# Attention with mixture of experts: one PSUM ring for scores and maxima, two heads' maxima in one instruction, a fourth v buffer, a new order

## The chip, the cores and the metric

The kernel runs on one core of a Trainium2 chip. Its time is the device time of one execution in microseconds; before the change it was measured three times. Engines are named as in the profile: PE (matrix products; PEld is its weight load), DVE, ACT, POOL, and SP, which issues most of the transfers.

## The reference, cut

```
q_n, k_n = rmsnorm(q, g_q), rmsnorm(k, g_k)          # 8 x 12 heads, 448 tokens, 64 wide
scores = q_n @ k_n.T / 8
scores = scores - max(scores)
attn = exp(scores) / (sum(exp(scores)) + 1e-9)
x = reshape(attn @ v)                                # 3584 tokens x 768
e_idx = argmax(x @ w_gate)                           # one of 8 experts for each token
gate_w = softmax(x @ w_gate)[e_idx]; eom = sigmoid(x @ w_output_gate)
for e in range(8):
    mask = e_idx == e
    ye = relu(x[mask] @ w1[e]) @ w2[e]               # 768 -> 1024 -> 768
    out[mask] = gate_w[mask] * eom[mask, e] * ye
```

All of it is f32. The kernel keeps that accuracy by splitting factors into a high and a low f16 part and adding three f16 products.

## The kernel before, in words

**Attention** runs over 48 pairs of heads (8 batches of 6). `pair_ops(i)` lists the steps of pair `i`; a letter and a number is the name of a step in the tables. Lt loads q and k; sq, mh, ms, n, qg norm them; hi and lo split them into f16 parts, Th and Tl turn them by DMA transposes (`flip`) into `ss`. M0 to M3 (line 548) multiply the high parts alone, each head's block of 128 rows by 448 columns into a bank of PSUM, and x0 to x6 (line 556) take the maxima of rows on DVE into `Z`. NT turns Z on PE, nt copies it out. S0 to S3 are the exact scores less the maximum, in four units of keys; e, f and p make the exponentials on ACT and split them (`ph` on ACT, `pl` on POOL or DVE). A *whole* unit keeps one f32 exponential `pf` instead; `WHOLE` says how many a pair has, by the pair's number modulo 6. Lv loads v, vh and vl split it. A0 to A6 multiply with v: for whole units one f32 product, for others three f16 products. av1, av2, av divide by the sums, tr, th, lg, la feed the gate, and `route(b)` then sorts a batch's tokens by expert: the table `tab` and rows of x, `xs`, go to HBM. The last row of xs is blank, written once by k.xs; k.tab fills the table first.

**PSUM** has eight banks: `ps_m` three single banks, for M, NT, routing and the tails; `ps_s` two double banks, for S and the experts' products; `ps_a` one.

**Order.** `Order.run()` writes the program of attention and of the first expert. For each engine it takes, among the steps whose predecessors and buffers (`BUFS`) are ready at a planned time, the one with the lowest key; keys come from the tables `ORDER` (for each step, and by the remainder of the pair) and `SHIFT`, planned durations from the calls of `do` and `add`, and `SECOND` says in which pairs a step runs on its second engine. Each engine then works through its own list in that order. A step waits there, and all behind it, until its data are there.

**Experts.** Job e multiplies the tokens of expert e: a main part of 384 tokens and a tail. Tokens are gathered (`xge`), split by ACT and DVE (`x16e`) and turned by DMA transposes (`xTe`). `wstream` loads weights in six pieces a job (`wste`, three buffers) and splits each twice: high part w0he or w1he on ACT, low part on DVE. g1 is the first product, `he0h`/`he0l` its rounded and low part (`he0th`, `he0tl` in the tail), g2 the second. All 12 splits of job 1 stand in the planned part, that is, ahead of the tail of job 0; later ones are interleaved with the products by `wstep`:

```
def wstep(k):
    if splits and splits[0][0] == k + 1:
        m, x = splits.pop(0)
        for w in range(2):
            split(m, x, w)
        if x % 2 and loads:
            load(*loads.pop(0))
```

Of the kernel before, what the change touches and what calls it, by code (L numbers as in the profile page):

```python
# [22 lines left out]
E, F = 8, 1024  # L23
# [15 lines left out]
WHC = 1024  # L39
LGN = 2  # L40
# [4 lines left out]
BUFS = dict(m=3, s=2, a=1, p32=3, ph=3, pl=2, pf=2, ss=4, X=3, Z=3, nt=3, vh=3, vl=3, xT=4, sq=2, qkt=8, vf=3, ms=2, y=2, xg=2, x16=2, o=2, lg=2, rt=2, wst=3, ti=4)  # L45
# [3 lines left out]
    ("Lt", -47.506, -68.244, 168.634),  # L49
    ("sq", 302.855, -337.037, 75.045),  # L50
    ("mh", -605.679, -57.018, -151.507),
    ("ms", 295.539, 1280.387, 511.843),
    ("n", 76.337, -596.069, 411.443),
    ("qg", 3.274, -959.675, 293.592),
    ("hi", 220.1, -124.186, -353.622),
    ("Th", -96.148, 38.457, 271.519),
    ("lo", -200.856, -181.461, -607.745),
    ("Tl", -323.414, -550.546, 270.775),
    ("M0", -2.62, -24.949, -432.815),
    ("x0", -103.535, 25.55, -15.932),  # L60
    ("x4", 106.174, 131.323, -155.443),
    ("M1", -1.058, 0.342, -5.456),
    ("x1", -145.398, -78.771, -73.078),
    ("x5", -20.548, 262.928, -60.28),
    ("M2", -1.178, 1.859, 2.292),
    ("x2", -278.017, -206.72, -471.808),
    ("x6", -75.108, -103.324, 28.323),
    ("M3", -1.508, 330.302, -654.327),
    ("x3", 278.734, -108.242, -87.117),
    ("NT", -116.679, 2.458, 167.319),  # L70
    ("nt", 38.455, -342.151, -44.891),
    ("S0", 0.304, -0.032, -203.657),
# [12 lines left out]
    ("e3", -41.908, 331.636, 270.381),
    ("f3", 191.382, 481.021, -45.813),
    ("p3", -148.41, 311.486, -229.907),
    ("Lv", -0.418, -102.362, 203.578),
    ("vh", -222.505, -41.76, 172.536),
    ("vl", -110.713, 163.718, -1030.872),  # L90
    ("A0", 2.002, 263.597, 250.508),
    ("A1", -1.073, -322.948, 280.671),
    ("A2", -14.914, -632.993, 316.303),
    ("A3", -34.425, -48.666, -54.49),
    ("A4", 1.105, -437.479, -191.275),
    ("A5", 1.7, -0.098, 256.361),
    ("A6", 1.506, 0.301, 308.556),
    ("av1", -171.058, -1206.521, -141.056),
    ("av2", -106.328, 26.761, -592.507),
    ("av", -154.077, -642.22, -844.834),  # L100
    ("tr", -108.772, -139.57, -75.908),
    ("th", -228.323, -289.618, -1169.065),
    ("lg", 4.374, -1.236, 520.21),
    ("la", -239.437, -568.368, 565.533),
# [10 lines left out]
STICK = 0.027  # L115
# [15 lines left out]
    "p0": "100001 111101 001010",  # L131
    "p1": "110111 111110 000101",
    "p2": "100010 000000 101001",
    "p3": "110111 111001 011110",
    "lo": "100000 000000 110110",
    "vh": "000000 000000 011111",
    "th": "011111 000100 110101",
    "n": "110010 010100 011101",
    "qg": "100000 000011 110100",
    "nt": "110100 011011 000100",  # L140
}

WHOLE = (1, 1, 2, 2, 1, 1)
# [3 lines left out]
IN_TURN = ("hi", "Th", "vh", "th")  # L147

SHIFT = {
    "k.cst": -322.738,  # L150
    "k.gd": -238.947,
    "k.wg": 285.318,
    "k.blank": 152.09,
    "k.xs": 825.387,
    "k.tab": 400.65,
    "k.g": 296.375,
    "k.ltri": 502.271,
    "k.flat": -263.51,
    "k.edges": -261.446,
    "s0": -499.19,  # L160
    "r": 0.991,
    "st": -373.362,
    "s": 218.895,
    "r-2": -262.274,
    "r-1": -937.938,
    "open1": -790.202,
    "open2": -304.552,
    "ld0": 240.548,
    "wh0": 191.816,
    "wl0": 143.296,  # L170
    "ld1": -708.071,
    "wh1": -407.871,
    "wl1": 164.604,
    "ld2": 302.394,
    "ti0": 81.591,
    "xg0": 97.719,
    "xh0": 401.873,
    "xl0": -377.394,
    "xt0": -242.315,
    "ti1": -167.525,  # L180
    "xg1": -77.39,
    "xh1": 234.09,
    "xl1": 344.869,
    "xt1": -204.364,
    "ti2": -606.745,
    "xg2": -196.244,
    "xh2": -377.672,
    "xl2": 151.592,
    "xt2": -439.307,
    "units": 8.951,  # L190
    "g1": 764.664,
    "hh": 366.746,
    "hl": -393.214,
    "g2": 394.253,
    "o0": -88.676,
    "o1": 471.038,
    "sc": -498.536,
    "k.sel": 435.503,
# [118 lines left out]
class Kern:  # L317
# [12 lines left out]
    def consts(self):  # L330
# [3 lines left out]
        self.ps_m = self.pool("ps_m", 3, PSUM)  # L334
        self.ps_s = self.pool("ps_s", 2, PSUM)
# [24 lines left out]
        z = c.tile([128, KD], F32, name="zrow")  # L360
# [27 lines left out]
        add("k.wg", SP, 475, [], -5.5, load(self.wg, io["wg"]), (), 2000, 400)  # L388
        add("k.blank", POOL, 900, [], -8, blank)
        add("k.xs", SP, 475, ["k.blank"], -3.5, load(self.xs[NT : NT + 1, :].rearrange("o (k p) -> (o p) k", p=128), z), (), 2000, 336)  # L390
# [4 lines left out]
        add("k.tab", SP, 475, ["k.blank"], -3, table, (), 2000, 742)  # L395
# [89 lines left out]
    def pair_ops(self, i):  # L485
# [227 lines left out]
        do("Lt", SP, 475, "", lambda: self.stat_load(i), "qkt:lo", 1650, 1150)  # L713
# [11 lines left out]
        do("Th", SP, 1235, "hi", lambda: flip(0), f"ss:{Ss},M0,M1,M2,M3 Z:NT", 1650, 1215, more=["k.edges"])  # L725
        eng, ns = engine("lo")
        do("lo", eng, ns, "hi", lambda eng=eng: lo(eng))
        do("Tl", SP, 1235, "lo Th", lambda: flip(1), "", 1650, 1215)
        for k in range(4):
            js = (k, k + 4) if k < 3 else (3,)  # L730
            do(f"M{k}", PE, 195 if k < 3 else 210, "Th", lambda js=js: M(js), " ".join(f"m:x{j}" for j in js))
            for j in js:
                do(f"x{j}", DVE, 531, f"M{k}", lambda j=j: x(j))
# [402 lines left out]
    def product(self, q, nm):  # L1136

        if not q["tail"]:
            return self.ps_s.tile([128, 2, 512], F32, tag="s", name=nm)[:, :, 0 : q["n"]]
# [368 lines left out]
```

## Time and profile before

| | |
|---|---|
| median of 3 runs | 1059.21 us (1058.59 to 1063.82) |
| profiled execution | 1063.45 us, its span 1061.6 us |
| busy PE, PEld | 963.3 us (91% of the span), 680.8 us |
| busy DVE, ACT, POOL | 652.2, 558.9, 422.5 us |
| mean granted clock of PE | 0.969 |

The profiled execution is one of its own, 4.24 us above the median. Busy times are of the engine's own instructions; a matmul that runs beside another one on other rows of the array is counted once. A share of busy time over the whole span hides stretches with other limits, so the span is read in pieces: attention to about 505 us, the change-over to about 647, then the experts. Where an instruction had to wait, the trace names the engine and line, or the transfer, that released it.

### The profile page before, as it was taken

What the parts mean: (1) busy time and instruction counts of PE and PEld (TensorE: products, weight loads), DVE (VectorE), ACT (ScalarE), POOL (GpSimd) and SP (SyncE); (2) the same over time, 40 slices, a digit from 0 to 9 for tenths busy, and PEclk for the clock granted to TensorE, in tenths of its full rate; (3) what the DMA queues carried; (4) which work ended last, traced back from release to release, by engine and by line L of the source; (5) the groups of instructions that cost most, each with busy time, mean ns of one, the idle gap of its engine ahead of it and who ended that gap; (6) DMA issues with size and microseconds to landing.
All of it is one profiled execution on the core that took longest, in us unless ns stands there. A gap on an engine that the chain in (4) does not pass through costs nothing. (4 is left out here: it accounts for less than half of the span.)

```text
span 1061.6 us, 27539 instructions
## 1 busy us (share of the span) xinstructions
PE 963.3 (91%) x11800; PEld 680.8 (64%) x11800; DVE 652.2 (61%) x1201; ACT 558.9 (53%) x876; POOL 422.5 (40%) x337
## 2 busy tenths in 40 slices
PE   0789999999899999999879959989999899999997
PEld 0457776767667777777556556676676666666664
DVE  5897988797887987788745443616416144354310
ACT  5686878778677786665543433404325143343310
POOL 6885586777667666344421311121111200101001
PEclk9799999999999999999989969999999999999999
DMA  9656757557584674737583883743828538386301
GB/s 233 139 121 130 192 129 160 131 108 195 98 183 101 157 158 82 144 62 138 130 147 132 254 271 117 208 160 111 235 74 224 181 97 233 108 218 209 99 15 44
DMA packets 183309, 157.32 MB, mean 148 GB/s; under 512 B 153226, under 2 KB 161034, under 8 KB 177040
## 3 DMA queue, kind: packets, MB, share of 16 engines
q1 hardware_dynamic: 177136, 131.18, 51.4%
q0 software_dynamic: 6048, 24.35, 7.1%
q8 instruction: 94, 1.54, 0.6%
q14 instruction: 31, 0.25, 0.1%
HBM read 96.73 MB, written 22.59 MB: 112 GB/s over the span
## 5 line engine op out<-in xcount | busy, mean ns | idle before, releaser
L557 DVE TENSOR_REDUCE Z<-psM 128x1 f16<-128x448 f32 x336 | 196.3, 615 | 30.9 <-PE psM L554 26.8
L579 PE MATMUL pss<-ss 64*128 64x448 f16 (+1 forms) x1152 | 152.9, 370 | 13.3 <-ACT p L597 6.4
L636 PE MATMUL psa<-vf,pf 128*128 128x65 f32 (+1 forms) x1024 | 160.7, 276 | 2.6 <-issue 2.6
L605 POOL TENSOR_TENSOR pl<-p,ph 128x896 f16<-128x896 f32 (+1 forms) x67 | 115.0, 1717 | 81.1 <-ACT p L597 40.5
L636 PEld LDWEIGHTS psa<-vf,pf 128*128 128x128 f32 (+1 forms) x1024 | 121.0, 178 | 31.3 <-issue 23.8
L1172 POOL DMA_INDIRECT out<-oe,tie x24 | 29.8, 1240 | 259.2 <-DVE oe L1194 203.8
L601 ACT ACTIVATE ph<-pss 128x896 f16<-128x896 f32 (+1 forms) x128 | 97.7, 774 | 57.6 <-PE pss L585 51.8
L538 POOL TENSOR_TENSOR X<-qkt,X 128x512 f16<-128x512 f32 x86 | 102.8, 1219 | 57.5 <-ACT X L534 57.4
L1157 PE MATMUL g1e<-xTe,w0he 128*128 128x384 f16 x384 | 125.2, 326 | 0.0
L1159 PE MATMUL g1e<-xTe,w0le 128*128 128x384 f16 x384 | 125.2, 326 | 0.0
L1158 PE MATMUL g1e<-xTe,w0he 128*128 128x384 f16 x384 | 125.2, 326 | 0.0
L640 PE MATMUL psa<-vh,pl 128*128 128x65 f16 (+1 forms) x1024 | 118.4, 195 | 1.1 <-issue 1.1
L640 PE MATMUL psa<-vh,ph 128*128 128x65 f16 (+1 forms) x1024 | 118.1, 196 | 0.0
L638 PE MATMUL psa<-vl,ph 128*128 128x64 f16 (+1 forms) x1024 | 117.9, 193 | 0.0
L554 PE MATMUL psM<-ss 64*128 64x448 f16 (+1 forms) x384 | 80.0, 372 | 37.7 <-DMA ss<-X 24.6
L640 PEld LDWEIGHTS <-ph 128*128 128x128 f16 (+1 forms) x1024 | 105.4, 118 | 0.1
L585 PEld LDWEIGHTS <-sel 64*128 64x128 f16 (+1 forms) x1536 | 64.5, 101 | 36.2 <-issue 6.3
L640 PEld LDWEIGHTS <-pl 128*128 128x128 f16 (+1 forms) x1024 | 85.9, 101 | 1.2 <-issue 1.2
L638 PEld LDWEIGHTS <-ph 128*128 128x128 f16 (+1 forms) x1024 | 85.7, 103 | 0.0
L1158 PEld LDWEIGHTS <-w0he 128*128 128x128 f16 x624 | 61.8, 100 | 35.3 <-issue 11.7
L579 PEld LDWEIGHTS <-ss 64*128 64x128 f16 (+1 forms) x1152 | 50.2, 100 | 52.4 <-issue 19.9
L1157 PEld LDWEIGHTS <-w0he 128*128 128x128 f16 x624 | 61.7, 100 | 28.0 <-DMA xTe0t<-x16e0t 2.3
(309 smaller groups left out, 2314.7 us busy)
## 6 DMA issues: line engine op xcount, KB each, us to landing
wste<-w SPq DMA_DIRECT2D x46, 1024.0 KB
qkt<-qkt SPq DMA_DIRECT2D x48, 448.0 KB
vf<-v SPq DMA_DIRECT2D x48, 260.0 KB
xs<-xr SPq DMA_DIRECT2D x16, 576.0 KB
wste<-w POOLq DMA_DIRECT2D x2, 1024.0 KB
ss<-X SPq DMA_TRANSPOSE x96
xs<-xr SPq DMA_DIRECT2D x16, 96.0 KB
tab<-val,slot POOLq DMA_INDIRECT x32
```

Source lines behind the costliest of these rows:

```text
L538: (V if eng == DVE else Pl).tensor_tensor(out=X[:, 1, :, :, d], in0=x, in1=X[:, 0, :, :, d], op=ALU.subtract)
L554: T.matmul(o[:, :S], lhsT=side(0, 0, h, c, n), rhs=side(0, 1, h, 0, S), start=True, stop=True)
L557: V.tensor_reduce(out=Z[:, 64 + j : 65 + j], in_=st[f"M{j}"][:, :S], op=ALU.max, axis=AX.X, negate=True)
L579: T.matmul(o[h], lhsT=side(wk, 1, h, 128 * u, n), rhs=side(wq, 0, h, 0, S), start=k == 0, stop=False)
L601: A.activation(out=t, in_=st[f"S{u}"], func=AF.Exp)
L605: (V if eng == DVE else Pl).tensor_tensor(out=t, in0=st[f"e{u}"], in1=st[f"ph{u}"], op=ALU.subtract)
L636: T.matmul(out, lhsT=st[f"pf{u}"][:, k, q], rhs=vf[:, jv, :], **go)
L638: T.matmul(out[:, 0:D], lhsT=st[f"ph{u}"][:, k, q], rhs=vl[:, jv, :], start=False, stop=False)
L640: T.matmul(out, lhsT=st[f"p{'hl'[w // 2]}{u}"][:, k, q], rhs=vh[:, jv, :], **go)
L1157: nc.tensor.matmul(o, lhsT=wh[:, sl], rhs=xT[:, 0, k, 0:n], start=k == 0, stop=False)
L1158: nc.tensor.matmul(o, lhsT=wh[:, sl], rhs=xT[:, 1, k, 0:n], start=False, stop=False)
L1159: nc.tensor.matmul(o, lhsT=wl[:, sl], rhs=xT[:, 0, k, 0:n], start=False, stop=k == KD - 1)
```

## The change

One ring of three double banks, `ps_s`, takes S, M, the routing and the tails' products; `ps_m` and `ps_a` have one bank each. An M step writes both heads' blocks into the two banks of one buffer, and one reduction takes both maxima. One unit fewer is whole in every sixth pair. v has four buffers. The tables of the order are all new (one row is shown), as are the planned times of four kinds of DMA. The blank row is written from six partitions in runs of 512 B, and with the table's first fill after pair 0's output. Of job 1's 12 splits eight stand in the planned part, the other four go through `wstep`.

```
-BUFS = dict(m=3, s=2, a=1, ..., vf=3, ...)
+BUFS = dict(m=1, s=3, a=1, ..., vf=4, ...)
+EARLY = 8
...
-    ("M0", -2.62, -24.949, -432.815),
+    ("M0", -1.393, -65.091, 0.926),
...
-STICK = 0.027
+STICK = 0
...
-WHOLE = (1, 1, 2, 2, 1, 1)
+WHOLE = (1, 1, 1, 2, 1, 1)
...
-        self.ps_m = self.pool("ps_m", 3, PSUM)
-        self.ps_s = self.pool("ps_s", 2, PSUM)
+        self.ps_m = self.pool("ps_m", 1, PSUM)
+        self.ps_s = self.pool("ps_s", 3, PSUM)
...
-        z = c.tile([128, KD], F32, name="zrow")
+        z = c.tile([KD, 128], F32, name="zrow")
...
-        add("k.xs", SP, 475, ["k.blank"], -3.5, load(self.xs[NT : NT + 1, :].rearrange("o (k p) -> (o p) k", p=128), z), (), 2000, 336)
+        add("k.xs", SP, 475, ["k.blank", "av.0"], 2, load(self.xs[NT : NT + 1, :].rearrange("o (k p) -> (o k) p", p=128), z), (), 2000, 60)
...
-        add("k.tab", SP, 475, ["k.blank"], -3, table, (), 2000, 742)
+        add("k.tab", SP, 475, ["k.blank", "av.0"], 2, table, (), 2000, 742)
...
-        def M(js):
-            for j in js:
-                ps = bank(f"M{j}")
-                for h in range(2) if j == 3 else [j // 4]:
-                    o = ps[64 * h : 64 * h + 64] if j == 3 else ps
-                    c, n = (0 if h else 384, 64) if j == 3 else (128 * j if j < 3 else 128 * j - 448, 128)
-                    T.matmul(o[:, :S], lhsT=side(0, 0, h, c, n), rhs=side(0, 1, h, 0, S), start=True, stop=True)
-        def x(j):
-            V.tensor_reduce(out=Z[:, 64 + j : 65 + j], in_=st[f"M{j}"][:, :S], op=ALU.max, axis=AX.X, negate=True)
+        def M(k):
+            ps = st[f"M{k}"] = self.ps_s.tile([128, 2, 512], F32, tag="s", name=f"psM{k}_{i}")
+            for h in range(2):
+                o = ps[:, h, :S] if k < 3 else ps[64 * h : 64 * h + 64, 0, :S]
+                c, n = (128 * k + 64 * h, 128) if k < 3 else (0 if h else 384, 64)
+                T.matmul(o, lhsT=side(0, 0, h, c, n), rhs=side(0, 1, h, 0, S), start=True, stop=True)
+        def x(k):
+            m = st[f"M{k}"][:, 0 : 2 if k < 3 else 1, :S]
+            o = Z[:, 64:72].rearrange("p (h j) -> p h j", h=2)[:, 0 : m.shape[1], k]
+            V.tensor_reduce(out=o, in_=m, op=ALU.max, axis=AX.X, negate=True)
...
-        do("Lv", SP, 570, "", lambda: self.loadv(i), f"vf:{As}", 1650, 720)
+        do("Lv", SP, 475, "", lambda: self.loadv(i), f"vf:{As}", 2100, 1200)
...
-            ps = self.ps_m.tile([128, 512], F32, tag="m", name=f"psl{b}")
+            ps = self.ps_s.tile([128, 2, 512], F32, tag="s", name=f"psl{b}")[:, 0]
...
-            for x in range(12 if m < 2 else 0):
+            for x in range((12, EARLY, 0)[m]):
...
-        splits = [(m, x) for m in range(2, E) for x in range(12)]
+        splits = [(m, x) for m in range(1, E) for x in range(12)][EARLY:]
```

Three places show what the new order moves. The first is DVE at the start, around the first maximum (L557 before, L556 now). `ms` sums squares, `y` and `psy` are the norm's factors, `qkt` the normed pair, `Z` the maxima. Before:

```order
L517 TENSOR_REDUCE ms_232<-sq_206 128x14
L467 SCALAR_TENSOR_TENSOR y_221<-psy_222,y_221 128x28
L521 TENSOR_TENSOR qkt_145<-qkt_145,y_221 128x896
L517 TENSOR_REDUCE ms_232<-sq_229 128x14
L557 TENSOR_REDUCE Z_109<-psM_0_243 128x1
L557 TENSOR_REDUCE Z_109<-psM_0_248 128x1
```

Now:

```order
L515 TENSOR_REDUCE ms_255<-sq_244 128x14
L470 SCALAR_TENSOR_TENSOR psy_251<-psy_251,mm_247 128x42
L465 SCALAR_TENSOR_TENSOR y_250<-psy_251,y_250 128x42
L519 TENSOR_TENSOR qkt_170<-qkt_170,y_250 128x896
L524 TENSOR_TENSOR qkt_158<-qkt_158,g 128x448
L515 TENSOR_REDUCE ms_255<-sq_262 128x14
L556 TENSOR_REDUCE Z_109<-psM_0_264 128x1
L556 TENSOR_REDUCE Z_109<-psM_0_269 128x2
```

The norms of later pairs (42 columns, three pairs' factors together) now stand ahead of the first maximum, which is row 31 of DVE now and was row 25.

The second is ACT at the end of attention, around the third `x16e` (the third block of the first expert's last tokens); `ph`, `p` and the `pss` in place are exponentials of the last pairs, `xT` copies for the gate, `w0he` splits of the first expert's weights. Before:

```order
L1119 ACTIVATE x16e_2_10775<-xge_10448 128x768
L601 ACTIVATE ph_1_10785<-pss_1_10743 128x896
L594 ACTIVATE pss_1_10743<-pss_1_10743 128x2x448
L601 ACTIVATE ph_3_10806<-pss_3_10760 128x448
L597 ACTIVATE p_3_10818<-pss_3_10760 128x448
L1054 ACTIVATE w0he_10426<-wste_2_10730 128x1024 x2
L601 ACTIVATE ph_2_10887<-pss_2_10836 128x896
```

Now:

```order
L600 ACTIVATE ph_2_10732<-pss_2_10706 128x896
L593 ACTIVATE pss_2_10706<-pss_2_10706 128x2x448
L495 ACTIVATE xT_118<-pstr_10727 128x448
L1116 ACTIVATE x16e_2_10793<-xge_10430 128x768
L495 ACTIVATE xT_119<-pstr_10795 128x448
L1051 ACTIVATE w0he_10432<-wste_2_10768 128x1024 x2
L1159 ACTIVATE he0h<-g1e_0_10946 128x768
```

The exponentials that stood behind that x16e stand ahead of it; one copy for the gate is left behind it.

The third is ACT at the hand-off from the first expert's main part to its tail. Before:

```order
L1119 ACTIVATE x16e_2_11593<-xge_11402 128x768
L1054 ACTIVATE w1he_11555<-wste_4_11558 128x1024 x2
L1054 ACTIVATE w1he_11555<-wste_5_11602 128x1024 x2
L1165 ACTIVATE he0th<-g1e0t_11629 128x288
L1165 ACTIVATE he0th<-g1e0t_11668 128x288
L1165 ACTIVATE he0th<-g1e0t_11707 128x288
L1165 ACTIVATE he0th<-g1e0t_11746 128x288
```

Now:

```order
L1051 ACTIVATE w1he_11426<-wste_4_11429 128x1024
L1159 ACTIVATE he0th<-g1e0t_11488 128x288
L1051 ACTIVATE w1he_11426<-wste_4_11429 128x1024
L1051 ACTIVATE w1he_11426<-wste_5_11472 128x1024
L1159 ACTIVATE he0th<-g1e0t_11533 128x288
L1051 ACTIVATE w1he_11426<-wste_5_11472 128x1024
L1159 ACTIVATE he0th<-g1e0t_11578 128x288
```

The last four splits of job 1 stood ahead of all roundings of the tail; now they alternate with them, and the last two roundings follow the last split.

## Rows read from the trace of the kernel before

**Rows 1.** Stretches: start:end, length, busy us (instructions) by engine, PEclk, DMA share, GB/s.
```profile
66.00:505.00 439.00, 421.60 (x7008) 316.35 (x7006) 366.38 (x784) 325.93 (x547) 279.01 (x204) 0.99 0.63 133
505.00:556.00 51.00, 38.56 (x600) 29.79 (x599) 31.19 (x52) 26.76 (x35) 16.93 (x13) 0.90 0.73 143
...
609.70:646.80 37.10, 22.98 (x289) 22.62 (x289) 11.35 (x14) 9.79 (x14) 8.10 (x7) 0.77 0.77 242
646.80:1061.60 414.80, 396.15 (x3219) 261.50 (x3216) 164.22 (x210) 135.16 (x179) 54.77 (x48) 0.99 0.49 145
```
**Rows 2.** Waits of PE, 66 to 505 us: total, times, longest.
```profile
PE psNT L562 <- DVE Z L557: 7.3, 9, 1.6
PE psM L554 <- ACT xT L497: 4.2, 4, 1.5
```
**Rows 3.** Timeline of PE: start, length of what is merged, instruction.
```profile
135.77 0.66 PE L636 MATMUL psa<-vf,pf 128*128 128x65 f32 x4
...
136.44 0.64 PE L636 MATMUL psa<-vf,pf 128*128 128x65 f32 x4
...
246.28 0.61 PE L554 MATMUL psM<-ss 64*128 64x448 f16 x2
...
252.88 0.41 PE L636 MATMUL psa<-vf,pf 128*128 128x65 f32 x2
...
253.40 0.41 PE L636 MATMUL psa<-vf,pf 128*128 128x65 f32 x2
...
255.31 0.35 PE L554 MATMUL psM<-ss 64*128 64x448 f16 x2
255.59 0.34 PE L636 MATMUL psa<-vf,pf 128*64 128x65 f32 x4
...
256.79 0.36 PE L554 MATMUL psM<-ss 64*128 64x448 f16 x2
256.99 0.73 PE L579 MATMUL pss<-ss 64*128 64x448 f16 x6
...
260.53 0.51 PE L554 MATMUL psM<-ss 64*128 64x448 f16 x2
```
**Rows 4.** Groups by line and form, 66 to 505 us: count, busy, mean ns, idle before.
```profile
L557 DVE TENSOR_REDUCE Z<-psM 128x1 f16<-128x448 f32 x293 | 171.5, 616 | 24.3 <-PE psM L554 20.3 <-remote 2.8
L517 DVE TENSOR_REDUCE ms<-sq 128x14 f32<-128x896 f32 x33 | 35.5, 1077 | 5.9 <-ACT sq L507 5.9
...
L601 ACT ACTIVATE ph<-pss 128x896 f16<-128x896 f32 x70 | 63.9, 914 | 46.5 <-PE pss L585 43.7 <-PE psM L554 2.4
...
L605 POOL TENSOR_TENSOR pl<-p,ph 128x896 f16<-128x896 f32 x48 | 91.6, 1909 | 57.8 <-ACT p L597 28.9 <-ACT ph L601 12.3 <-issue 7.0
```
**Rows 5.** The head: timeline of SP's queue and DVE, then DMA of 17.5 to 21.5.
```profile
16.16 1.34 SPq L542 DMA_TRANSPOSE ss<-X  x1
...
24.95 1.16 DVE L557 TENSOR_REDUCE Z<-psM 128x1 f16<-128x448 f32 x2 [4.32 <-PE psM L554]
...
DMA packets 576, 0.14 MB, mean 34 GB/s; under 512 B 576, under 2 KB 576, under 8 KB 576
...
q1 hardware_dynamic: 576, 0.14, 118.5%
```
**Rows 6.** End of attention: timeline of SP's queue, ACT and PE.
```profile
531.73 19.23 SPq L1132 DMA_TRANSPOSE xTe<-x16e  x3
...
543.92 0.84 ACT L1119 ACTIVATE x16e<-xge 128x768 f16<-128x768 f32 x1 [8.34 <-DMA xTe<-x16e]
...
547.32 1.30 PE L579 MATMUL pss<-ss 64*128 64x448 f16 x6 [5.91 <-ACT p L597]
```
**Rows 7.** Hand-off to the tail: timeline of ACT, PE and DVE.
```profile
626.80 2.00 ACT L1054 ACTIVATE w1he<-wste 128x1024 f16<-128x1024 f32 x2 [8.30 <-DMA wste<-w]
628.71 0.99 ACT L1165 ACTIVATE he0th<-g1e0t 128x288 f16<-128x288 f32 x3
...
630.67 0.28 PE L1157 MATMUL g1e0t<-xTe0t,w0he 128*128 128x144 f16 x1 [10.45 <-DVE he0tl L1167]
...
635.63 0.46 DVE L1167 SCALAR_TENSOR_TENSOR he0tl<-g1e0t,he0th 128x288 f16<-128x288 f32 x1 [4.28 <-ACT he0th L1165]
```

More of the change, by code (lines that the diff above doesn't have):

```diff
@@ new lines @@
+    ("x1", -0.424, -203.998, 733.194),
+    ("M2", -1.519, -45.398, 19.977),
+    ("x2", -173.664, 715.115, 578.71),
+    ("M3", -2.656, -184.071, 11.601),
+    ("x3", -162.741, -249.796, -263.98),
+    ("NT", -30.754, -292.604, 48.932),
+    ("nt", -99.651, -386.223, 353.695),
+    ("S0", -0.011, 1.674, 4.547),
+    ("e0", 424.663, 55.28, 152.539),
+    ("f0", -389.187, -24.305, -889.411),
+    ("p0", 182.287, -43.502, 707.229),
+    ("S1", -0.302, 1.053, -103.987),
+    ("e1", -44.729, -1349.511, -397.429),
@@ L141 @@
+    "lo": "100000 000000 000001",
+    "vh": "010011 000000 110110",
+    "th": "100001 000010 010010",
+    "n": "010010 010100 110101",
+    "qg": "001000 000010 100100",
+    "nt": "101000 001100 100000",
 }
-WHOLE = (1, 1, 2, 2, 1, 1)
+WHOLE = (1, 1, 1, 2, 1, 1)
 HALVED = 6
-IN_TURN = ("hi", "Th", "vh", "th")
+IN_TURN = ("hi", "Th", "vh", "tr", "th")
 SHIFT = {
[L150 to L198, printed above, removed]
@@ new lines @@
+    "k.cst": -714.614,
+    "k.gd": -558.236,
+    "k.wg": 345.674,
+    "k.blank": 212.539,
+    "k.xs": 1050.584,
+    "k.tab": 184.575,
+    "k.g": -99.124,
+    "k.ltri": 447.207,
+    "k.flat": -367.328,
+    "k.edges": -566.262,
+    "s0": -292.117,
+    "r": -96.746,
+    "st": -768.984,
+    "s": 221.695,
+    "r-2": -433.645,
+    "r-1": -899.652,
+    "open1": -853.45,
+    "open2": 95.138,
+    "ld0": 286.328,
+    "wh0": 268.421,
+    "wl0": -80.449,
+    "ld1": -630.158,
+    "wh1": -732.659,
@@ new lines @@
+    "wl1": 121.704,
+    "ld2": 883.59,
+    "ti0": 364.023,
+    "xg0": -180.498,
+    "xh0": 422.318,
+    "xl0": -422.478,
+    "xt0": 313.506,
+    "ti1": 395.469,
+    "xg1": 228.098,
+    "xh1": 293.3,
+    "xl1": 455.297,
+    "xt1": 266.788,
+    "ti2": -23.541,
+    "xg2": -199.273,
+    "xh2": -399.549,
+    "xl2": -63.85,
+    "xt2": -156.53,
+    "units": 191.688,
+    "g1": 1019.317,
+    "hh": 703.057,
+    "hl": -312.59,
+    "g2": -62.563,
+    "o0": 442.161,
+    "o1": 227.865,
@@ L199 @@
+    "sc": -98.894,
+    "k.sel": 892.663,
 }
@@ L895, in line @@
                 first = nm
-        add("first", PE, 107, " ".join(f"la.{i}" for i in pairs if i % LGN == LGN - 1), first, [("rt", [f"{g}z{c}" for c in range(NC)]), ("m", [g + "ex", g + "zz"])])
+        add("first", PE, 107, " ".join(f"la.{i}" for i in pairs if i % LGN == LGN - 1), first, [("rt", [f"{g}z{c}" for c in range(NC)]), ("s", [g + "ex", g + "zz"])])
         line(
@@ L1136, in product @@
     def product(self, q, nm):
-        if not q["tail"]:
-            return self.ps_s.tile([128, 2, 512], F32, tag="s", name=nm)[:, :, 0 : q["n"]]
-        ps = self.ps_m.tile([128, 512], F32, tag="m", name=nm)
-        return ps[:, 0 : 2 * TW].rearrange("p (a t) -> p a t", a=2)[:, :, 0 : q["n"]]
+        return self.ps_s.tile([128, 2, 512], F32, tag="s", name=nm)[:, :, 0 : q["n"]]
     def g1_units(self, q):
@@ L1291, in moe @@
         for m in range(3):
-            for j in range(6 if m < 2 else BUFS["wst"]):
+            for j in range(6 if m < 2 else EARLY // 2 - 6 + BUFS["wst"]):
                 pool = (0, 2) <= (m, j) < (0, 4)
@@ L1347, in moe @@
         plan = self.plan()
-        loads = [(m, j) for m in range(2, E) for j in range(6)][BUFS["wst"] :]
-        splits = [(m, x) for m in range(2, E) for x in range(12)]
+        loads = [(m, j) for m in range(2, E) for j in range(6)][EARLY // 2 - 6 + BUFS["wst"] :]
+        splits = [(m, x) for m in range(1, E) for x in range(12)][EARLY:]
         def wstep(k):
```

137 lines of the change are left out of this document (57 added, 80 removed).

## The prediction

> **What bounds the kernel now.** I read the busy times by stretch first [rows 1]. From 66 to 505 us, the steady part of attention, PE is busy 421.6 of 439 us, against 366 on DVE, 326 on ACT and 279 on POOL: PE sets the pace there and stands idle for 17.4 us. In the last stretch, the expert products, it is busy 396 of 415. The poor stretches lie between: 505 to 556, where attention ends and the first expert's tokens are fetched (12.4 of 51 us idle, clock 0.90), and 609.7 to 646.8, the tail of the first expert (14.1 of 37.1 us idle, clock 0.77). A shorter time must therefore come from less PE work in attention, or from those two places. The waits of PE in the steady part [rows 2] come next: the longest is the small transpose of the maxima, NT, behind DVE's maximum, 7.3 us over nine times; then M behind ACT, 4.2. So the maxima are the only place where DVE holds PE up at all.
>
> **The change part by part.** The profiled execution took 1063.45 us, 4.24 above the median of 1059.21. I sum against the first and take 4.24 off at the end.
>
> *One whole unit instead of two, in 8 of 48 pairs.* A whole unit keeps one f32 exponential, and its product is f32. Groups of A in a pair with two such units start 0.67 us apart (135.77 to 136.44), with one 0.52 apart (252.88 to 253.40) [rows 3]. At 0.13 to 0.15 a group, 7 groups and 8 pairs make 7.3 to 8.4 us. One of the eight is pair 2, in the head, where PE waits in any case, and the seventh group is a half one, so I take **−6** (bounds −5 and −8.4). What replaces it lies off the path: a ph pass on ACT, 0.91 us, and a pl on POOL, 1.91 [rows 4], eight times each, 7 and 15 us beside slack of 113 and 160 [rows 1].
>
> *M's two heads in one double bank.* Before, each head's block takes a bank of its own, and where the second one waits for a bank the two no longer run side by side. In the timeline of PE I count 21 such couples between 66 and 511 us. Two of them: at 246.28 and 260.53 they span 0.61 and 0.51 us, where a joined couple at 256.79 spans 0.36 [rows 3]. 0.15 to 0.25 each is 3.2 to 5.3 us; I take **−4**. Afterwards both halves have one buffer and one wait.
>
> *Order of PE.* Between shapes PE loses a little: from an M couple to A's it is 0.28 us (255.31 to 255.59), to S of the same shape 0.20 (256.79 to 256.99) [rows 3]. Changes of shape along PE's order number 503 before and 465 now; 38 by 0.08 is **−3** (bounds 0 and −3.6, since a change next to a wait costs nothing).
>
> *The maxima.* Seven reductions of 448 columns, 0.616 us each, become three of 896 and one of 448. No row has an 896-wide reduction out of PSUM; the nearest is the one over squares, 1.077 us [rows 4]. From that, 7 x 0.616 = 4.31 us a pair become 3.85: DVE gains 0.46 us a pair, at most 22 in all, and PE does not see it as work. The other side is the ring. A double bank is held 1.08 us by its maximum, where a single was held 0.62, and M now shares three double banks with S. The seats are as many as before, but a late exponential on ACT now keeps M out too. That price stands in no row. Below, a gain is possible: all of the NT and M waits, 11.5 us [rows 2], could go, of which I allow −8. Above, 144 double maxima held 0.46 us longer are 66 us, of which nearly all hides in the slack between buffers; I bound it at a bit over a third, +25, and take **+3**, near the low end, because in the rows the waits for a maximum are short, 0.8 us a time.
>
> *Fourth v buffer, other planned DMA times, other second engines.* No DMA is among PE's waits of any size in the steady part [rows 2], so 0, covered by the buffers of qkt and v; were that cover gone, the loss would lie within the ring's upper bound. What moves between DVE, POOL and ACT lies in their slack of 73 to 160 us: 0. The tails' products have three buffers as before, double now: 0.
>
> *The head.* The blank row of xs, 4 bytes a packet, moves behind pair 0's output, with the table's first fill. In 17.5 to 21.5 us this transfer holds the queue at 118.5% for 0.14 MB, and the transpose issued at 16.16 ends late; DVE's first maximum starts at 24.95 [rows 5]. But the order of DVE now puts two reductions of squares and three wider steps of pairs 5 to 7 ahead of that maximum, and ACT's first rounding stands before the last square they need. So it starts at some 25 to 26 us whatever the DMA does: **0** (bounds −4 and +4). The Trainium skill, page "DMA: Bandwidth & Descriptors", section Specifications, gives 512 B as the smallest transfer at line rate; 768 packets of 4 B become 6 of 512 B. This case's rows agree that small packets are slow (34 GB/s). If that alone decided, the head would gain its 4 us and the time would be 1036.
>
> *End of attention.* Before, ACT's third x16e waits 8.34 us for a buffer that transposes of xTe hold, and the exponentials of the last pairs stand behind it; PE stops 5.91 us at 547.32 waiting for p [rows 6]. Now all but one of ACT's steps of attention stand ahead of that x16e, so this stop goes. What is late next is the chain of the last tokens: routing, gather, x16e and the transposes, of which three alone take 19.23 us [rows 6]; it sets the start of the products at 556 and is not shortened. I take **−4** (bounds 0 and −12.4, all idle time of the stretch).
>
> *Hand-off to the first tail.* ACT issues four splits of the next weights, two waiting 8.30 us for their load, and three roundings he0th stand behind them; PE stops 10.45 us [rows 7]. Now the splits alternate with the roundings. The last roundings still follow split 10, whose weights come at 626.8 as before, because SP's order there is the same. Split 10, a rounding, split 11, two roundings and their he0tl, from 626.80 on, at about 1.0, 0.33, 1.0, 0.66 and some 1.8 more, end near 631.6, where the last he0tl ended at 636.1 [rows 7]. **−5** (bounds 0 and −16: the 10.45, and 5.3 for the 22.98 us of PE work at clock 0.77). The two loads that now follow wait for the same buffers as before: 0.
>
> Sum: −6 −4 −3 +3 +0 −4 −5 = −19, to 1044.4 for an execution like the profiled one, 1040.2 on the median: **1040**.
>
> **The rivals.** *The gains are given back.* If DVE and ACT, not PE's work, set the length of attention once PE is shorter, the 13 us of the first three terms turn into waits: −6 is left, 1053; if the chain of the last tokens holds too, 1057. For it: NT already waits for DVE. Against it: DVE has 73 us of slack [rows 1].
>
> *The ring turns against it (slower).* PE waits at each double maximum for the third buffer. The point from which this decides is where the waits reach 22 us instead of 3, a third of the 66; at half of it, 33, the time is 1070. For it: M and S come through one queue of buffers, so a late exponential delays maxima. Against it: a buffer's next user follows about two microseconds after the earlier one in the order, and a maximum takes 1.08.
>
> *The clock.* PE's short stops in a stretch come with a lower clock: 505 to 556 was granted 0.90, against 0.99 from 66 to 505 [rows 1]. Were the steady part to go to 0.90, 439 x 0.09 = 40 us would be lost, 1080. The Trainium skill, page "TensorE: Matmul & The Clock Gate", section "A second HAM failure mode: psum-queue depth-cycling", tells of just this: PE idles for moments as it cycles through PSUM buffers, and the clock falls and rises. The trace agrees only in part: the kernel before cycles so already and is granted 0.99.
>
> *More goes than I allow.* The hand-off's wait and its low clock vanish, −16 instead of −5, and the end of attention gives 12 instead of 4: 1021. For it: both stops have one engine's order as cause, and that order is rewritten.
>
> *The change does not do what it says* can't be for banks and maxima, which are written out; for the measured DMA times it can, and costs nothing in the sum.
>
> **How the numbers follow.** A measurement of this kernel can tell about 0.5% from no change: 1053.9 and 1064.5 are the borders. Forecast, 1022 to 1053: 0.62. More: 0.16. Given back, 1054 to 1064: 0.11. Ring: 0.07; clock: 0.04. Faster 0.78, same 0.11, slower 0.11. The range reaches from 1018, a little below the case of more, to 1062; outside it lie the slower cases and the far ends of the others, some 0.18.
>
> **What would show it.** In the profile after: A's groups 0.52 apart in the third of every six pairs too; couples of M side by side, none torn; the stretch to 505 shorter by about 10, with PE's idle time there still near 20 us; double maxima near 1.08 us; no stop at p before the last x16e; the stop in the tail near 5 us. Wrong it would be if M waits for S's exponentials by tens of us, if the reduction from PSUM takes well over 1.1 us, if NT waits longer than the 7.3, or if the steady clock falls below 0.97.

## The result

| | before | changed |
|---|---|---|
| median of 19 runs | 1062.5 us (1058.18 to 1068.12) | 1048.91 us (1045.07 to 1058.09) |
| ratio, 95% interval | | 0.9875 (0.9851 to 0.9898) |
| profiled execution, span | 1063.45, 1061.6 us | 1047.8, 1046.2 us |
| busy PE, DVE, ACT, POOL | 963.3, 652.2, 558.9, 422.5 us | 944.6, 632.2, 565.6, 447.6 us |

The change takes 13.6 us, where 19 were forecast; the time lies in the stated range. To compare stretches I cut both traces at the same events: the output of the sixth and of the 42nd pair, the end of the first expert's main part and of its tail. The busy times by stretch of the kernel before (start:end, length, busy us of PE, PEld, DVE, ACT, POOL, granted clock, DMA share, GB/s):

```profile
0.00:113.47 113.47, 77.16 (x1058) 51.87 (x1058) 90.55 (x162) 79.01 (x136) 82.03 (x78) 0.92 0.68 156
113.47:495.81 382.34, 366.43 (x6060) 273.98 (x6058) 318.56 (x679) 284.91 (x482) 245.85 (x181) 0.99 0.63 133
495.81:609.73 113.92, 100.60 (x1187) 70.85 (x1180) 67.50 (x139) 50.07 (x67) 31.77 (x24) 0.96 0.69 171
609.73:646.99 37.26, 23.14 (x291) 22.75 (x291) 11.35 (x14) 9.79 (x14) 8.10 (x7) 0.77 0.77 241
646.99:1061.60 414.61, 395.96 (x3216) 261.38 (x3214) 164.22 (x210) 135.16 (x179) 54.77 (x48) 0.99 0.49 145
```

And of the changed one:

```profile
0.00:112.27 112.27, 72.18 (x1084) 49.16 (x1084) 93.82 (x140) 81.37 (x138) 87.34 (x86) 0.98 0.67 164
112.27:478.49 366.22, 349.50 (x6056) 262.87 (x6055) 300.40 (x562) 285.71 (x473) 257.72 (x189) 0.99 0.62 137
478.49:596.34 117.85, 104.56 (x1224) 74.81 (x1224) 61.03 (x127) 52.68 (x71) 39.73 (x30) 0.93 0.59 156
596.34:629.39 33.05, 21.58 (x289) 21.43 (x290) 12.75 (x16) 10.87 (x16) 5.31 (x5) 0.85 0.86 264
629.39:1046.20 416.81, 396.81 (x3217) 263.07 (x3214) 164.20 (x210) 134.96 (x179) 57.47 (x52) 0.98 0.49 148
```

Down to the end of the main part (three rows), PE's busy time falls from 544.2 to 526.2 us, by 18.0; its idle time (length less busy) rises from 65.5 to 70.1, by 4.6. The tail gives 4.2, the rest takes 2.2 back. These are one profile of each kernel; where other profiles of the same order differ, the part on the prediction says so. In the steady row PE idles 15.9 us before and 16.7 after: the work went, the waits stayed. Which waits they are has changed [rows 2]:

```profile
PE pss L578 <- DVE pl L604: 4.4, 5, 1.0
...
PE psNT L561 <- DVE Z L556: 1.9, 8, 0.3
PE psNT L561 <- DVE lg L686: 1.9, 3, 0.8
```

DVE's maxima hold NT up for 1.9 us where it was 7.3; M's waits behind ACT are gone, and S now waits 4.4 us for DVE's low parts, which was 0.8. The last line is new in kind. NT needs nothing of `lg`, the gate's sums that DVE copies out of PSUM; but NT, the gate's products, the transposes `pstr` ahead of them and the norm's `psy` all take their buffers from `ps_m`, which the change cut from three banks to one. NT waits there for the bank. The double maximum out of PSUM, which no row of before showed, takes as long as the reduction of squares did [rows 4]:

```profile
L556 DVE TENSOR_REDUCE Z<-psM 128x2 f16<-128x896 f32 x124 | 131.4, 1082 | 19.3 <-PE psM L551 18.9
L515 DVE TENSOR_REDUCE ms<-sq 128x14 f32<-128x896 f32 x33 | 35.2, 1068 | 12.4 <-ACT sq L505 12.4
```

The three other places. The head, PE before, then PE and DVE now [rows 5]:

```profile
24.36 1.07 PE L554 MATMUL psM<-ss 64*128 64x448 f16 x4 [24.36 <-DMA ss<-X]
...
30.43 0.37 PE L562 MATMUL psNT<-id,Z 128*128 128x128 f16 x2 [1.68 <-DVE Z L557]
```

```profile
19.24 1.44 PE L551 MATMUL psM<-ss 64*64 64x448 f16 x6 [19.24 <-DMA ss<-X]
...
26.82 1.61 DVE L556 TENSOR_REDUCE Z<-psM 128x1 f16<-128x448 f32 x2
...
27.49 0.56 PE L551 MATMUL psM<-ss 64*128 64x448 f16 x2 [6.80 <-DVE Z L556]
...
34.22 0.37 PE L561 MATMUL psNT<-id,Z 128*128 128x128 f16 x2 [1.55 <-DVE y L465]
```

M starts 5.1 us earlier, its maximum 1.9 us later, and the first NT comes at 34.22, where it came at 30.43. NT's own wait there, 1.55 us, is again for the one bank of `ps_m`: `y` is what DVE computes from `psy`. The end of attention, ACT and PE [rows 6]:

```profile
531.56 0.84 ACT L1116 ACTIVATE x16e<-xge 128x768 f16<-128x768 f32 x1 [7.48 <-DMA xge<-xs,tie]
...
533.94 0.54 ACT L495 ACTIVATE xT<-pstr 128x448 f32<-128x448 f32 x1
...
534.53 1.11 PE L663 MATMUL pstr<-cst,xr 128*128 128x128 f32 x4 [5.57 <-ACT xT L495]
```

The stop at the exponentials, 5.91 us, is replaced by one of 5.57: a copy xT stands behind the second x16e, which waits 7.48 us for gathered rows, and the next `pstr` can't start before xT has emptied the bank of `ps_m`. And the hand-off [rows 7], the start of the tail on PE before, then PE and ACT now:

```profile
611.66 0.24 PE L1157 MATMUL g1e0t<-xTe0t,w0he 128*128 128x144 f16 x1 [1.93 <-DMA xTe0t<-x16e0t]
```

```profile
601.87 0.28 PE L1151 MATMUL g1e0t<-xTe0t,w0he 128*128 128x144 f16 x1 [5.54 <-DMA xTe0t<-x16e0t]
...
615.76 1.06 ACT L1051 ACTIVATE w1he<-wste 128x1024 f16<-128x1024 f32 x1 [7.00 <-DMA wste<-w]
616.72 0.39 ACT L1159 ACTIVATE he0th<-g1e0t 128x288 f16<-128x288 f32 x1
...
618.50 0.28 PE L1213 MATMUL g2e0t<-he0th,w1he 128*128 128x144 f16 x1 [5.93 <-DVE he0tl L1161]
```

The 10.45 us stop is 5.93 now, behind split 10, which waits 7.00 us for its load. In its place PE waits longer at the start of the tail, for the tail's own transposes.

### The profile page after: what moved, and what is told of

Its sections match the earlier page's. It is cut to its first block, busy times and chain, and to the rows that moved or that the text cites. A ratio compares the mean times of both kernels' runs of the same rounds, so it can differ in the third digit from the quotient of the medians.

```text
span 1046.2 us, 27627 instructions
## 1 busy us (share of the span) xinstructions
PE 944.6 (90%) x11864; PEld 671.3 (64%) x11864; DVE 632.2 (60%) x1054; ACT 565.6 (54%) x874; POOL 447.6 (43%) x358
## 4 chain that ended last, share of the span: by engine, by line
PE 39%; issue 15%; DMA 7%; DVE 6%; ACT 1%; POOL 1%; POOLq 1%; another core or an unknown queue 0%; SPq 0%; DVEq 0%; ACTq 0%
PE psa L635 4%; PE pss L578 4%; PE g1e L1151 3%; PE g1e L1153 3%; PE g1e L1152 3%; PE g2e L1201 3%; PE g2e L1200 3%; PE g2e L1199 3%; PE psa L639 2%; DVE Z L556 2%; DMA out<-oe,tie 1%; PE psM L551 1%; DMA tab<-val,slot 1%; PE pss L584 1%; PE pstr L663 1%
## 5 line engine op out<-in xcount | busy, mean ns | idle before, releaser
L556 DVE TENSOR_REDUCE Z<-psM 128x2 f16<-128x896 f32 (+1 forms) x192 | 180.9, 966 | 28.9 <-PE psM L551 28.4
L604 POOL TENSOR_TENSOR pl<-p,ph 128x896 f16<-128x896 f32 (+1 forms) x74 | 123.3, 1671 | 79.4 <-ACT ph L600 31.6
L635 PE MATMUL psa<-vf,pf 128*128 128x65 f32 (+1 forms) x896 | 149.8, 280 | 4.0 <-ACT pf L590 1.1
L635 PEld LDWEIGHTS psa<-vf,pf 128*128 128x128 f32 (+1 forms) x896 | 110.0, 180 | 28.3 <-issue 19.8
L600 ACT ACTIVATE ph<-pss 128x896 f16<-128x896 f32 (+1 forms) x136 | 106.8, 789 | 30.9 <-PE pss L584 30.3
L536 POOL TENSOR_TENSOR X<-qkt,X 128x512 f16<-128x512 f32 x92 | 110.0, 1218 | 28.7 <-ACT X L532 21.2
L639 PEld LDWEIGHTS <-ph 128*128 128x128 f16 (+1 forms) x1088 | 111.4, 118 | 0.6 <-issue 0.6
L551 PE MATMUL psM<-ss 64*128 64x448 f16 (+1 forms) x384 | 67.9, 376 | 31.7 <-DMA ss<-X 19.5
L637 PEld LDWEIGHTS <-ph 128*128 128x128 f16 (+1 forms) x1088 | 91.7, 104 | 1.2 <-issue 1.2
L1151 PEld LDWEIGHTS <-w0he 128*128 128x128 f16 x624 | 61.8, 100 | 34.1 <-issue 10.5
L1153 PEld LDWEIGHTS <-w0le 128*128 128x128 f16 x624 | 61.8, 100 | 27.7 <-issue 2.9
```

The source lines that it names most:

```text
L536: (V if eng == DVE else Pl).tensor_tensor(out=X[:, 1, :, :, d], in0=x, in1=X[:, 0, :, :, d], op=ALU.subtract)
L551: T.matmul(o, lhsT=side(0, 0, h, c, n), rhs=side(0, 1, h, 0, S), start=True, stop=True)
L556: V.tensor_reduce(out=o, in_=m, op=ALU.max, axis=AX.X, negate=True)
L600: A.activation(out=t, in_=st[f"S{u}"], func=AF.Exp)
L604: (V if eng == DVE else Pl).tensor_tensor(out=t, in0=st[f"e{u}"], in1=st[f"ph{u}"], op=ALU.subtract)
L635: T.matmul(out, lhsT=st[f"pf{u}"][:, k, q], rhs=vf[:, jv, :], **go)
```

## The experiments

Twelve runs in three sets, each set on one chip (the chip differs between them), with the kernel before beside it. A ratio is to the kernel before of the same set, a difference of times within a set.

**First set.** Parts undone, and one part alone; before stood at 1049.83 us. *Two whole units again*, the order kept; in `e`, `f`, `p` and the product:

```
+        kept = range(2 if i % 6 == 2 else WHOLE[i % 6])
-            if u in whole:
+            if u in kept:
```

> The changed kernel with its order kept, but two units instead of one are whole again in the third of every six pairs (eight pairs). Theory (the work taken from PE carries the gain): PE is busy 6 to 8 us longer in all, nearly all of it in attention, and the time rises by 5 to 8 us, to 1054 to 1057 where the change stands at 1048.9. Rival (ACT and DVE set the pace of the new order): PE's extra work fits into its waits, and the sixteen passes saved on ACT pay for it: within 2 us of 1048.9.

*One maximum for each head*, the order and the banks kept:

```
-            V.tensor_reduce(out=o, in_=m, op=ALU.max, axis=AX.X, negate=True)
+            for h in range(m.shape[1]):
+                V.tensor_reduce(out=o[:, h : h + 1], in_=m[:, h, :], op=ALU.max, axis=AX.X, negate=True)
```

> The changed kernel with its order and its banks, but each double maximum is two reductions of 448 columns again. DVE is then busy longer by about 48 x 3 x (2 x 0.616 - 1.08) = 22 us, and each double bank is held 0.15 us longer. Theory (DVE has slack, the ring is roomy): waits of PE for a maximum in the steady part grow by 1 to 4 us, time 1050 to 1053. Rival (one instruction for two heads is what made the ring fit): waits for maxima grow by 10 us or more, time above 1058.

*The splits as before*, `EARLY = 12` in the changed kernel:

> The changed kernel with all 12 splits of the second expert's weights ahead of the first tail's roundings on ACT again; nothing else in any engine's order moves. Theory: the stop before the second expert's products comes back, some 10 us in place of 5.9, with more of the tail at the low clock; the stretch from the end of the first expert's main part to the end of its tail goes from 33 to 38 to 41 us and the time to 1053 to 1057. Rival (the tail waits for its tokens, not for ACT's order): the stretch stays within 1.5 us of 33.

*The splits alone*, `EARLY = 8` with its four lines in `moe` in the kernel before:

> The kernel before with this part of the change alone: four of the 12 splits alternate with the first tail's roundings on ACT. Theory: the 10.45 us stop in the tail shrinks by 4 to 6 us and part of the low clock with it; the stretch of 37.3 us becomes 29 to 33, the time 1055 to 1058 where before stands at 1062.5. Rival (the load of the last weights sets the end whatever the order): within 1.5 us of 1062.5.

Measured: 1017.72 us (0.9715, 0.967 to 0.9759), 1021.23 (0.9747, 0.9701 to 0.9793), 1019.55 (0.9736, 0.9689 to 0.9782), and for the splits alone 1046.27 (0.9946, 0.9904 to 0.9988). All three times of the changed kernel are far below 1048.9, and so is before: the absolute numbers expected are void, and a measure on the same chip was missing. Inside the set one reading holds: the third kernel is the changed one down to the tail. Against it, attention and main part (from the start to the end of g2's main part) are longer by 6.0 us with two whole units (586.97 to 580.95) and by 9.2 with single maxima (590.11). NT's wait for maxima between 66 and 490 us is 5.1 in place of 3.5. That growth of 1.6 is what was expected of the waits. Of the 9.2 us some 3 are idle time of PE in the steady part; most of the rest is PE busy longer where its granted clock was lower (0.96 in the head and 0.90 at the end of attention, against 0.99 and 0.94). So the one instruction for two heads is worth some us of the time, at a place where I had reckoned none; how many, this set can't say. Its rival's 10 us of waits do not appear. The 6.0 us of the two whole units are mixed with the clock in the same way; the third set repeats them. With the splits as before the tail's stretch takes 39.5 us, against 35.9 and 35.7 in the two kernels beside it, at the middle of what was expected; the stop is 7.58 us and not some 10, and 8.07 us of waiting for the transposes stand ahead of it. The splits alone give 0.5%, some 5 us (the interval: 1 to 10), as expected; but in its profile the stop is still 7.29 us and the tail's stretch 34.3, where 29 to 33 were expected, so the profile doesn't show where those 5 us lie.

**Second set**, with the changed kernel as a measure; before stood at 1075.4 us.

> The changed kernel itself, beside the runs of this call and on their chip: the runs before this one stood at 1049.8 us for the kernel before where the first measurement had 1062.5, so what each undone part costs has to be read against the changed kernel on the same chip. Theory (what differs between the sets of runs is the chip, and it acts on both kernels): the ratio to the kernel before is 0.980 to 0.990 and the last stretch, after the first tail, takes the same time as in the other runs of the set. Rival (the change gains more where PE is fed faster): the ratio is 0.965 to 0.975.

*The first pair's maxima ahead* on DVE; after the order is planned, steps are moved in the list:

```
+ M3.0 M1.0 M0.0 M2.0 behind Th.0;  x3.0 x1.0 behind n.1;  x0.0 x2.0 behind ms.6
```

> The changed kernel with one thing moved: DVE takes the four maxima of the first pair as soon as M has written them, ahead of the squares of pairs 4 to 7. Theory (the head's loss is DVE's order): PE's 6.8 us stop after the first M's shrinks to under 2 us, NT comes at 27 to 29 us in place of 34.2, and the time falls by 3 to 6 us. Rival (the pairs that follow are late in its place): idle time of PE up to the sixth pair's output stays within 1.5 us, and so does the time.

*The second x16e behind the copy*:

```
+ xh0.1 xl0.1 xt0.1 behind p2.47
```

> The changed kernel with one thing moved: at the end of attention the second x16e on ACT (with its low part on DVE) goes behind the last exponentials and one copy xT, which it held up by 7.5 us. Theory (the chain of the last tokens sets the start of the expert's products): PE's stop of 5.6 us goes, but the products start only 0 to 3 us earlier, since the last gathered rows and their transposes come as before; time down by 0 to 3. Rival (PE's work sets it): the start moves by 5 us or more and the time falls by 5 to 10.

*Two late splits in the tail's second product*:

```
-                for u in self.g1_units(q):
+                for f, u in enumerate(self.g1_units(q)):
                     act(u)
-                    wstep(k)
+                    if k or f < 2:
+                        wstep(k)
```

> The changed kernel with only two of the four late splits in the first product of the first tail and two in its second product, so that all four roundings stand ahead of split 10 and its wait for the load. Theory: the 5.9 us stop ahead of the tail's second product goes, with part of the low clock; the tail's stretch falls by 4 to 8 us and the time by as much. Rival (the weights come late and hold the next job up): what is gained there is lost after it, time within 1.5 us.

Measured: control 1055.1 us (0.9826, 0.9776 to 0.9876); first maxima 1057.73 (0.9841, 0.9805 to 0.9877); copy ahead 1053.41 (0.9803, 0.9764 to 0.9843); late splits 1046.33 (0.9736, 0.9693 to 0.978). The control's ratio is in the range expected, and its last stretch takes 420.8 us where the three others take 419.7 to 420.6.

The theory on the head falls. In the timeline of PE and DVE of that kernel the maximum comes at once, and the stop moves to the next pair's transposes:

```profile
19.42 1.44 PE L551 MATMUL psM<-ss 64*64 64x448 f16 x6 [19.42 <-DMA ss<-X]
20.77 1.61 DVE L556 TENSOR_REDUCE Z<-psM 128x1 f16<-128x448 f32 x2
...
28.98 1.44 PE L551 MATMUL psM<-ss 64*64 64x448 f16 x6 [6.98 <-DMA ss<-X]
...
35.61 0.37 PE L561 MATMUL psNT<-id,Z 128*128 128x128 f16 x2 [2.30 <-DVE y L465]
```

NT is at 35.61, later than before the move: in PE's order it stands behind the second pair's M's, which wait for their own transposes until 28.98 (28.48 in the control). All maxima of the first pair are done at 27.01; NT's last 2.30 us go to `psy`, which holds the one bank of `ps_m` until DVE has read it. PE's idle time up to the sixth pair's output is 42.9 us against 40.0 in the control, and the time is no shorter: neither the theory nor its rival. Moving DVE alone could not bring NT forward; moving PE's NT with it, or ahead of `psy`, was not tried. The copy ahead lies within the noise, and its profile can't be read against the control's: the gathered rows landed at other times in each. In the control the second x16e waits only 2.05 us, and there is no stop of 5.6 to take away (the longest is 3.41, of the gate's product behind a copy xT); with the copy ahead 2.52 of that is left, and the products start at 548.1 where they start at 540.4 in the control. In two other profiles of the unmoved order, the one of the result and the first maxima's, they start at 547.1 and 548.5. What the move is worth stays open. The late splits do what was expected: the stretch of the tail goes from the first row (control) to the second:

```profile
589.62:625.45 35.83, 22.70 (x290) 22.53 (x290) 13.57 (x17) 10.87 (x16) 7.66 (x6) 0.81 0.90 263
```

```profile
591.49:618.97 27.48, 21.02 (x289) 20.86 (x290) 12.94 (x16) 10.98 (x16) 3.88 (x3) 0.88 1.05 306
```

The stop ahead of the tail's second product is 1.29 us, where the control's is 5.20. The stretch is 8.4 us shorter, and the last stretch takes the same time in both (420.6 and 420.8), so the rival, that it is lost again after the tail, falls. The medians are 8.8 us apart, with spreads of 14 and 19 us over six runs each, and the intervals of the two ratios just overlap: that there is a gain over the changed kernel is likely, its size in time is the less certain one. No other kernel of this set is faster.

**Third set**; before stood at 1045.25 us. *The changed kernel*, *two whole units* (edit as above), *the old table of steps* (ORDER of before without the rows of x4 to x6, all else as changed), and *the head's transfers alone* (in the kernel before: the 512 B runs, and k.xs and k.tab behind av.0).

> The changed kernel itself once more, beside the three runs that follow, as their measure. From the sets so far its ratio to the kernel before is 0.98 to 0.99 where the last stretch takes 415 to 421 us, and about 0.965 where it takes 397: I expect one of the two.

> The changed kernel with two whole units again in the third of every six pairs and its order kept, now with the changed kernel on the same chip. Theory (PE's work): attention up to the end of the first expert's main part 5 to 7 us longer and the time 3 to 7 us longer than the changed kernel's. Rival (it fits into waits): within 1.5 us.

> The changed kernel with the table of steps (the 50 or so rows of ORDER) of the kernel before, without its rows for x4 to x6; banks, double maxima, the other tables and all else as changed. Theory (the parts take work from PE, the order keeps its waits short): PE's busy time stays within 6 us of the changed kernel's, its idle time in attention grows by 15 to 50 us, and the time is 1 to 5% above the changed kernel's, at or above the kernel before. Rival (the structure alone carries the gain): within 5 us of the changed kernel.

> The kernel before with this part alone: the blank row in runs of 512 B, and it and the table's first fill after the first pair's output; no other engine's order moves. Theory (in the order before, the head waited for that transfer; in the changed one it waits for DVE): the first M comes at 19 to 20 us in place of 24.4, the first NT at 25 to 28 in place of 30.4, PE's idle time up to the sixth pair's output falls by 2 to 5 us, and the time by as much. Rival (the head is DVE's either way): idle time there within 1 us.

Measured: control 1014.59 us (0.9711, 0.9676 to 0.9746), its last stretch 396.6, the gain a little smaller than I expected with it; two whole units 1019.13 (0.9746, 0.971 to 0.9783), 4.5 above it; the old table 1078.03 (1.0343, 1.0292 to 1.0394), some 6% above it, more than the 1 to 5 that I expected, and 3% above the kernel before; the head's transfers alone 1039.37 (0.9954, 0.9923 to 0.9985), 5.9 below before.

Two whole units cost PE what the rows of before said: the time that PE is at work on the products A, from the start into the tail (the first figure behind the length), in the control and then with two units:

```profile
0.00:596.00 596.00, 207.12 (x4160) 108.46 (x896) 36.98 (x96) 0.98 0.67 152
```

```profile
0.00:601.00 601.00, 214.98 (x4096) 120.80 (x1024) 36.99 (x96) 0.98 0.68 152
```

7.9 us. But most of it fits into waits: from the start to the end of the first expert's main part PE is busy 8.1 us longer and the stretch only 2.4 (583.6 against 581.25), where 5 to 7 were expected. Another 2.3 us lie in the tail (37.1 against 34.8), which this edit doesn't touch and which differs by as much between profiles of one kernel. So of the 4.5 us of time about half is the whole units', as far as these two profiles tell. The old table, by stretch (to the sixth, to the 42nd pair's output):

```profile
0.00:130.77 130.77, 79.30 (x1098) 54.41 (x1098) 97.36 (x142) 82.09 (x139) 90.20 (x86) 0.92 0.59 144
130.77:518.67 387.90, 358.46 (x6054) 269.03 (x6053) 312.17 (x560) 285.15 (x473) 256.12 (x190) 0.98 0.61 127
```

PE idles 51.5 and 29.4 us there, where the control, by its own rows,

```profile
0.00:111.80 111.80, 73.62 (x1084) 49.60 (x1084) 93.88 (x140) 81.38 (x138) 87.50 (x86) 0.97 0.66 164
111.80:465.66 353.86, 343.50 (x6056) 259.98 (x6055) 305.07 (x561) 285.76 (x473) 257.14 (x189) 1.00 0.67 141
```

idles 38.2 and 10.4, and PE is busy 21 us longer for the same work, of which the lower clock (0.92 and 0.98 against 0.97 and 1.00) may be up to 15; whether the 6 us that I allowed hold can't be told. The waits came as expected. So with a table that was made for the other structure the new one carries no gain. The reverse, a new table with the old banks, was not run: how much of the gain a new order alone would bring stays open. With the head's transfers alone, M starts at 19.22 and NT at 25.87, in the order of before: that transfer did hold the head up.

## Why the prediction was right, and where its sizes were off

*Whole units: −6.* Right as PE's work: its time on A falls by 7.0 us between the first two profiles (rows under the next point), and the experiment, at equal clock, gives 7.9. As time it was too much: undone, they lengthen the stretch by 2.4 us and the run by 4.5.

*Torn couples and changes of shape: −4 and −3.* The mechanism is right, the size is not. No torn couple of M is left, of 21; there is none with the old table either, so this is the shared bank's doing. PE's time on A, S and M (rows in that order, PE's time first, then that of the other engines that touch the tile) from the start into the tail, before, and then after:

```profile
0.00:611.60 611.60, 218.77 (x4096) 121.04 (x1024) 37.17 (x96) 0.97 0.65 145
...
0.00:611.60 611.60, 187.55 (x2688) 50.45 (x61) 245.78 (x320) 0.97 0.65 145
...
0.00:611.60 611.60, 79.97 (x384) 196.34 (x336) 0.97 0.65 145
```

```profile
0.00:601.80 601.80, 211.78 (x4160) 110.00 (x896) 37.02 (x96) 0.97 0.63 147
...
0.00:601.80 601.80, 178.97 (x2688) 53.69 (x62) 250.23 (x328) 0.97 0.63 147
...
0.00:601.80 601.80, 67.86 (x384) 180.90 (x192) 0.97 0.63 147
```

−8.6 on S and −12.1 on M. They overlap at their edges, and all of PE's work in that stretch falls by 18.0, A's 7.0 of it; so by subtraction some 11 us belong to these two terms, where I had 7, up to 3.4 of it the clock (an estimate, half of 37.5 less 30.7 us: of its two levels, 1.2 and 2.4 GHz, PE was granted the low one for 37.5 us there before and for 30.7 after). The old table with the new banks has 182.87 on S and 70.81 on M, at a clock of 0.96: most of what M lost is there without the new table, of what S lost about half. The split between banks and order is no closer than that, as the chip and the other tables differ too. I priced a change of shape by one place, M to A against M to S; what it costs elsewhere I didn't measure.

*The ring: +3.* Right in kind, +0.8 in the steady row. But the ring took its banks from `ps_m`, and that price stands nowhere in the sum: in the profile after, PE waits some 10 us from the start to the end of the main part for that one bank (5.57 behind xT, 1.9 behind `lg`, 1.55 behind `y`, and small ones), in the profile before for none of these. What a second bank there would give back was not run. That the maxima are the only place where DVE holds PE up was not quite so before, with 0.8 us of S behind `pl`, and is wrong now: `pl` is the longest wait. The double maximum has the length taken from the squares, 1.08 us. The rivals of the ring and of the clock did not come: waits of M for maxima stay below 1 us in the steady part, and the clock is 0.99 there as before.

*The maxima on DVE: no gain seen by PE.* Wrong by some us: undone, NT waits 1.6 us longer and PE idles some 3 us more in the steady part.

*The head: 0.* This is the step that failed. That DVE would not begin before 25 to 26 was right (26.82). But I took the end of the head as unchanged, where the same order also spreads the other maxima, and PE's idle time up to the sixth pair's output rises from 36.3 to 40.1. Alone, in the old order, the transfers of the head do gain: 0.5% of the time, M 5.1 us earlier and 2.0 us less idle time up to the sixth pair (34.3). In the new order it is lost again: to DVE's squares ahead of the first maximum, and with the maxima moved ahead of them to the second pair's transposes and to `psy` in the one bank that NT needs. The Trainium skill, page "DMA: Bandwidth & Descriptors", section Specifications, gives 512 B as the smallest transfer at line rate. The gain is in line with it but doesn't show it: the same edit also moves the transfer out of the head, and no run here did one without the other. Which order would keep both gains is open: the one move tried left NT behind the second pair on PE.

*End of attention: −4.* Too much: idle time from the 42nd pair's output to the end of the main part is 13.3 us in both profiles. Over all profiles the two orders overlap: 13.3, 14.7 and 16.4 with the order of before, 9.8 to 13.5 in five with the changed one, a gain of some 2 us on average. I named the chain of gather and transposes as next, and rightly, but looked at the third x16e alone; the second one waits for the same chain, with a copy behind it on which, with one bank in `ps_m`, PE's next step hangs.

*Hand-off: −5.* Right about the stop, 5.93 us where I had said near 5. That the stretch came out at −4.2 was in part luck, as the other profiles show (us; the wait at the start is for the tail's transposes, the stop is the longest behind ACT's roundings):

| profile | job 1's splits to the first tail's roundings | wait at its start | stop | stretch |
|---|---|---|---|---|
| before | 12 ahead | 1.93 | 10.45 | 37.3 |
| the head's transfers alone | 12 ahead | 0.49 | 12.50 | 33.2 |
| the splits alone | 8 ahead, 4 between | 4.21 | 7.29 | 34.3 |
| after; the two controls | 8 ahead, 4 between | 5.54; 7.94, 6.48 | 5.93; 5.20, 5.66 | 33.1; 35.8, 34.8 |
| the splits as before | 12 ahead | 8.07 | 7.58 | 39.5 |
| late splits | 8 ahead, 2 between, 2 behind | 5.17 | 1.29 | 27.5 |

The stop is shorter in every profile with fewer splits ahead of the roundings. What it gives is mostly taken back at the start, where the sum had nothing: the tail's last transpose was issued 5.8 us ahead of the main part's end before (603.93 to 609.73), and 1.0 us ahead of it after (595.38 to 596.34). That the rest of the stop is ACT's order is shown by the late splits.

Sum by stretches: −18.0 of work, +4.6 of waits, −4.2, +2.2: −15.4 between the two profiles, −13.6 between medians. That this comes near the −19 is in part luck: PE's work fell by 5 us more than the 13 of the sum, and that stands against 3.8 us more idle time in the head and the 4 us that didn't come at the end of attention. On the chip of the third set it is −30.7.

## What to carry to other kernels

When one engine is at work 96% of a stretch, count its work by shape and neighbour, for all places and not for one: what order and banks save there came through, while each stop that was removed elsewhere was replaced, in part or whole, by another behind a late transfer. When one user of PSUM gets more banks, list who lost them: the steps left on one bank wait for each other's readers. Before pricing a removed stop, list everything on that queue that stands behind an instruction waiting for the same data. And steps that wait for a load belong behind those that only wait for the engine next door: that one edit made its stretch 8.4 us shorter.

## What the runs showed of the hardware

The same program runs at two paces. In the first runs and the second set the last stretch takes 415 to 421 us, in the other two sets 396 to 397. About half of the difference is idle time (19 to 21 us against 8 to 9). There PE waits for nothing that the trace shows, in many small pieces; the costliest of them in the control of the second set, from 630 us on:

```profile
PE g1e4t L1151 <- issue: 1.8, 3, 0.9
PE g1e3t L1151 <- issue: 1.8, 3, 1.1
```

In all they are about 9 to 10 us; in the control of the third set there is none. The other half is PE busy longer with the same products, 396 to 401 us against 388, with 12 to 28 us at the low level of its clock against 4 in the third set's control. On the chip of the third set, one of the faster ones, the changed kernel gains more: 0.9711 against 0.9826 and 0.9875. Its steady part goes from 366.2 to 353.9 us, with 10.4 us idle instead of 16.7, while that of the kernel before with its head's transfers moved still takes 380.4. Why the old order does not profit was not tried, nor what makes one set slower than another. Two kernels have to be compared on one chip.
